# The order of ScalarE's copies where one PSUM bank is carried on into a second and a third

## The chip, the core and the metric

The kernel runs on one core of one Trainium2 chip. The metric is the device time of the whole program in microseconds (us), the median over runs. The core has five engines with queues of their own that work in program order: TensorE (PE in the profile; its weight loads are PEld), VectorE (DVE), ScalarE (ACT), GpSimd (POOL) and SyncE (SP, which here only issues DMA transfers). They wait for each other through semaphores.

## The reference

One sequence of 2048 positions and width 512 goes through a layernorm; its result feeds two branches, an attention over 8 keys at a distance of 2 with 32 heads, and a wide layer with a squared ReLU whose SiLU gates the first:

```python
xn = _layernorm(x)                               # [1, 2048, 512]
q, k, v = split(xn @ wqkv)                       # 32 heads of 16
idx = pos[:, None] - (jnp.arange(8) * 2)[None]   # keys at 0, -2, ... -14
attn = softmax(mask(q . k[idx]) * 16 ** -0.5)
s = (attn . v[idx]) @ wo
h = relu(xn @ w1 + b1) ** 2                      # width 1792
g = silu(h @ w2 + b2)
return x + s * g
```

Everything is float32.

## The kernel before

**Products.** TensorE multiplies float32 in a reduced form, so each operand is kept as a high part (ScalarE's copy into the reduced type) and a low part (VectorE's or GpSimd's subtraction of the high part from the operand), and each product is three passes: high by high, high by low, low by high. In the profile `xt`, `ss`, `w` and `h` are such pairs: a row `xt<-pxT` on ScalarE makes a high part, a row `xt<-pxT,xt` on VectorE the low one.

**Stages.** The 2048 rows are 16 tiles of 128. In the first stage each tile is normalised (`norm`, writes `xn`), spread over the partitions by four DMA transfers on SP (`shuffle`, `xb<-xn`), transposed on VectorE (`trans`, writes `pxT` for an even tile and `xs` for an odd one) and split into `xt`; then q, k and v are computed from it and stored to DRAM. The attention reads q, k and v from there and runs almost entirely on VectorE. The second stage runs the wide layer and the output product over four chunks of 512 rows. The order on all engines is written out by hand: every engine call goes through one helper on line 85, so that nearly all rows of the profile have this line and are told apart by their tiles. Attention steps are put in between by `pump`, which compares running estimates of TensorE's and VectorE's time when the program is built.

**Seven products instead of eight.** The tiles in pairs (a, a + 1) with a = 4, 6, 8, 10, 12 (`SEVEN`, line 41) compute v in the plain way (`qkv(t, 2)`, 12 matmuls, tile `pq`), but q and k together by seven products of half the depth (`seven`, line 562), 6 matmuls each. The left sides are two halves of `xt` and four sums of them, `ss`; the right sides are the weights `wq` and four sums of weights, `t`. GpSimd forms the sums of x (`sum_x`: `xs`, `xd`), after VectorE's first difference `xd<-pxT,xs`; `sum_high` (line 506) copies them to `ss` on ScalarE, and `sum_low` makes the low parts.

A first product is needed in several results. It is therefore computed once in bank X, and X is copied by ScalarE into bank Y when it holds one product and goes on by itself; Y takes another product and is copied into bank Z. These two copies are the forks of the banks. TensorE's order in a block is: X (first product, 6), v of tile a (`pq`, 12), the last product Z of the block before, X (second product, 6), v of tile a + 1 (12), Y, U, Z, Y (6 each). X's second product may not begin before the copy to Y has read the bank, and Z's product not before the copy to Z has written it.

**What stands on ScalarE beside this.** Block a also normalises tiles a + 4 and a + 5 (`first_norm`, line 738, and `second_norm`, line 742; `norm` is on line 437), as long as these exist, that is for a = 4 to 10. For tiles 6 to 15 the normalisation is one ScalarE instruction, `xn<-x,shift,rs`; its `shift` comes from GpSimd, and it writes the only buffer of `xn`, from which the four transfers of the pair before must have been read. After the second one `shuffle` issues the four transfers, and each normalisation is followed by a load of a later x on SP. `trans(t)` (line 469) ends with the copy that makes the high part of `xt`. The order around the forks is

```python
        product(X, x(a, 0), wq[0], start=True)
        first_norm(a)
        Y = psH(f"Y{a}")
        A.activation(Y, X, AF.Copy)
        second_norm(a)
```

and, further down, `trans(b + 2)` (line 605) in front of Y's next product and the copy to Z (line 609).

Of the kernel before, what the change touches and what calls it, by code (L numbers as in the profile page):

```python
# [40 lines left out]
SEVEN = range(4, 13, 2)  # L41
# [14 lines left out]
def body(ctx: ExitStack, tc: tile.TileContext, x, wqkv, wo, w1, b1, w2, b2, out):  # L56
# [48 lines left out]
    def psA(name):  # L105
        return psum.tile([P, 512], F32, name=name, tag="acc", bufs=4)

    def psH(name):
        return psum.tile([P, 512], F32, name=name, tag="h", bufs=2)

    def psT(name):
        return psum.tile([P, 512], F32, name=name, tag="tp", bufs=2)

    def piece(name):
        return keep.tile([P, 512], F32, name=name, tag="z", bufs=4)
# [248 lines left out]
    def pump(margin=-SLACK):  # L364

        limit = clock["PE"] + margin
        flush(clock["PE"])
        while True:
            if coming[0] is None:
                coming[0] = next(stream, None)  # L370
            if coming[0] is None or clock["V"] + coming[0] > limit:
                break
            coming[0] = next(stream, None)
        if coming[0] is None:
            not_before(limit)
# [61 lines left out]
    def norm(t):  # L437

        src = xins.pop(t)
        if t < TURN:  # L440
            xn[t] = dst = px.tile([P, 2, D], F32, name=f"xn{t}", tag="xb", bufs=2)[:, 0]
        else:
            if t % 2 == 0:
                xn[t] = px.tile([P, 4, 2, P], F32, name=f"xn{t}", tag="xn")
            dst = xn[t // 2 * 2][:, :, t % 2].rearrange("p a (k c) -> p k a c", k=KT)
            src = src.rearrange("p (k a c) -> p k a c", a=4, k=KT)
        if t < 6:
            halves = [slice(0, D // 2), slice(D // 2, D)] if t == 0 else [slice(None)]
            for i in halves:
                V.tensor_scalar(dst[:, i], src[:, i], mv[t][:, 0:1], rs[t], op0=OP.subtract, op1=OP.mult)  # L450
        else:
            A.activation(dst, src, AF.Identity, bias=shifts.pop(t), scale=rs[t])
        if t + 4 < NT:
            load_x(t + 4)

    def place(t):
        if t < TPC:
            xt[t] = xT[0][:, t]
        else:
            xt[t] = pxT.tile([P, 2, KT, P], FR, name=f"xt{t}", tag="xt", bufs=4)  # L460

    def shuffle(t):

        src = xn.pop(t)
        xb[t] = px.tile([P, 4, 2, P], F32, name=f"xb{t}", tag="xb", bufs=2)
        for a in range(4):
            dma(xb[t][32 * a:32 * a + 32].rearrange("p b e c -> p b (e c)"), src[:, a].rearrange("p e c -> p (e c)"))  # L467

    def trans(t):
        place(t)  # L470
        pTs[t] = piece(f"xs{t}") if t % 2 and t - 1 in SEVEN else psT(f"pxT{t}")
        if t < TURN:
            for kt in range(KT):
                PE.transpose(pTs[t][:, kt * P:(kt + 1) * P], xn[t][:, kt * P:(kt + 1) * P], ident)
            seen[t] = clock["PE"] + 800
        else:

            V.transpose(out=pTs[t].rearrange("p (k n b) -> p b k n", k=KT, b=4),
                        in_=xb[t // 2 * 2][:, :, t % 2].rearrange("p b (k c) -> p b k c", k=KT))
            seen[t] = clock["V"] + 800  # L480
        A.activation(xt[t][:, 0], pTs[t].rearrange("p (k n) -> p k n", k=KT), AF.Copy)

    def lowx(t):
        not_before(seen.pop(t))
        V.tensor_sub(xt[t][:, 1], pTs[t].rearrange("p (k n) -> p k n", k=KT), xt[t][:, 0].bitcast(F32))
        if t not in SEVEN and t - 1 not in SEVEN:
            pTs.pop(t)
# [3 lines left out]
    def sum_x(a):  # L491

        xe, t = pTs.pop(a), pTs.pop(a + 1)
        u = piece(f"xd{a}")
        V.tensor_sub(u, xe, t)
        sums[a] = t, u
        n = D // 2
        lo, hi = slice(0, n), slice(n, D)
        G.tensor_add(t[:, lo], t[:, lo], t[:, hi])
        G.tensor_sub(t[:, hi], t[:, hi], u[:, lo])  # L500
        G.tensor_add(u[:, hi], u[:, lo], u[:, hi])

    def four(ap):
        return ap.rearrange("p (s k n) -> p s k n", s=2, n=P)

    def sum_high(a):
        ss[a] = [pss.tile([P, 2, 2, 2, P], FR, name=f"ss{a}_{i}", tag="ss", bufs=2) for i in range(2)]
        for t, d in zip(sums[a], ss[a]):
            A.activation(d[:, :, 0], four(t), AF.Copy)

    def sum_low(a):
        for t, d, eng in zip(sums.pop(a), ss[a], (V, G)):
            eng.tensor_sub(d[:, :, 1], four(t), d[:, :, 0].bitcast(F32))
# [3 lines left out]
    def qkv(t, s, between=None, late=False):  # L517

        ps = (psH if t < 2 and s == 2 else psA)(f"pq{t}_{s}")
        order = [(kt, a, b) for kt in range(KT) for a, b in PASSES]  # L520
        if late:
            order.sort(key=lambda o: o[1])
        for n, (kt, a, b) in enumerate(order):
            PE.matmul(ps, xt[t][:, a, kt], wq[2 * s + kt // 2][:, b, kt % 2, :], start=n == 0, stop=n == 11)
            if between and n == 5:
                between()
        evacuate(t, s, ps)
# [9 lines left out]
    def store(t, s, stg):  # L537
        r0 = t * P + (0 if s == 0 else HALO)
        dst = (sq, sk, sv)[s][:, r0:r0 + UP, :].rearrange("g (p e) c -> p g (e c)", e=2)
        dma(dst, stg.rearrange("p g e c -> p g (e c)"))  # L540
        done = done_tiles["qkv"[s]]
        done[0] = t + 2
        done[1][t // 2] = clock["PE"]
# [18 lines left out]
    def seven(a):  # L562

        b = a + 1
        for s in (2, 0, 1):
            stgs[s] = pstg.tile([P, 4, 2, P], F32, name=f"stg{a}_{s}", tag="stg", bufs=5)
        sq_, sk_ = stgs[0], stgs[1]

        def x(t, h):
            return lambda p, k: xt[t][:, p, 2 * h + k]  # L570

        def s(i):
            return lambda p, k: ss[a][i // 2][:, i % 2, p, k]

        def product(ps, left, w, start=False, stop=False):
            n = 0
            for k in range(2):
                for p, r in PASSES:
                    PE.matmul(ps, left(p, k), w[:, r, k], start=start and n == 0, stop=stop and n == 5,
                              skip_group_check=True)  # L580
                    n += 1

        def groups(ps):
            return ps.rearrange("p (g c) -> p g c", g=4)

        X = psA(f"X{a}")
        product(X, x(a, 0), wq[0], start=True)
        first_norm(a)
        Y = psH(f"Y{a}")
        A.activation(Y, X, AF.Copy)  # L590
        second_norm(a)
        pump(LATE)
        qkv(a, 2)
        sum_high(a)
        pump(LATE)
        while tail:
            tail.pop()()
        product(X, x(a, 1), wq[1], stop=True)
        A.activation(sq_[:, :, 0], groups(X), AF.Copy, scale=0.25)
        sum_low(a)  # L600
        trans(a + 2)
        pump(LATE)
        qkv(b, 2)
        lowx(a + 2)
        trans(b + 2)
        pump(LATE)
        product(Y, s(1), tw[T2])
        Z = psH(f"Z{a}")
        A.activation(Z, Y, AF.Copy)
        U = psA(f"U{a}")  # L610
        product(U, s(0), tw[T1], start=True, stop=True)
        A.activation(sk_[:, :, 0], groups(U), AF.Copy)
        lowx(b + 2)
        if a + 2 in SEVEN:
            sum_x(a + 2)
        next_stats(a)
        pump(LATE)
        product(Z, s(2), tw[T3])
        product(Y, s(3), wq[3], stop=True)
        pump(1500)  # L620
        V.tensor_add(sk_[:, :, 1], groups(Z), sk_[:, :, 0])
        V.tensor_add(sk_[:, :, 0], groups(Y), sk_[:, :, 0])
        store(a, 1, sk_)

        def last():
            product(Z, x(b, 1), tw[T4], stop=True)
            A.activation(sq_[:, :, 1], groups(Z), AF.Copy, scale=0.25)
            store(a, 0, sq_)

        tail.append(last)  # L630
# [107 lines left out]
    def first_norm(a):  # L738
        if a + 4 < NT:
            norm(a + 4)  # L740

    def second_norm(a):
        if a + 4 < NT:
            norm(a + 5)
            shuffle(a + 4)

    def next_stats(a):
        if a + 6 < NT:
            for t in (a + 6, a + 7):
                mean(t)  # L750
                spread(t)

    for a in range(2, NT, 2):
        b, more = a + 1, a + 2 < NT
# [240 lines left out]
```

## Time and profile before

| | |
|---|---|
| median of 3 runs | 494.86 us (493.64 to 496.76) |
| the profiled execution | 495.17 us, span 493.2 us |
| first stage, by TensorE's rows | up to about 149 us of the span |
| blocks of seven, first X of each | 42.1, 60.9, 76.5, 92.1, 108.1 us |
| TensorE's granted clock, mean | 0.994 |
| waits on TensorE in the whole span | 3.3 (X for ACT's Y), 1.4 (Z for ACT's Z), 1.4, 0.4 and 0.2 us (at the start) |

A row of the timeline gives the start and the duration in us, the engine, the line, the operation, what is written and what is read (without buffer numbers), shapes and count, and, in brackets, the idle time of that engine before it with what ended it. Rows of equal neighbours are merged, so a row of six matmuls is one product. The durations of matmuls are printed with the tail of the last one. The view of the waits gives for each pair who waited and for whom, with the total, the number and the longest. The stretches by window show each engine's busy time, with the number of instructions, in a stretch of the span, and behind them the clock that TensorE was granted.

### The profile page before, as it was taken

The page shows a single profiled execution, that of the slowest core. Times are in us where ns is not written, and L with a number is a line of the kernel's source. Part 1 is how long each engine was busy: PE and PEld are TensorE (multiplying, and loading weights), DVE is VectorE, ACT ScalarE, POOL GpSimd, SP SyncE. Part 2 cuts the span into 40 slices and gives each one's busy share as a digit, 9 for nine tenths or more (in the row PEclk, how much of TensorE's full clock was granted, in tenths as well). Part 3 has the DMA queues.
Part 4 walks back from the last instruction along what each step waited for, and adds up shares of the span by engine and source line. Part 5 has one row for each costly group of instructions (what it writes and reads, how often), then busy time and mean ns, then how long its engine had stood idle before and what let it go on. Part 6 is the DMA issues. An engine that isn't in the chain of part 4 may idle for free.

```text
span 493.2 us, 5911 instructions
## 1 busy us (share of the span) xinstructions
PE 482.5 (98%) x2124; PEld 396.9 (80%) x2124; DVE 434.4 (88%) x370; ACT 227.1 (46%) x400; POOL 170.1 (34%) x149
## 2 busy tenths in 40 slices
PE   8997999999999999999999999999999999999996
PEld 5885778778888888888888888888888888888885
DVE  5996689899986999999999999899999969999543
ACT  5674555735265667229322423752233273424340
POOL 1325336422377899404140222140332213221100
PEclk9999899999999999999999999999999999999999
DMA  8799786798679964464336407471704643350222
GB/s 278 239 290 325 216 266 198 230 350 309 197 250 339 227 233 111 157 217 161 85 95 193 160 1 252 131 214 41 245 26 161 249 126 84 127 139 22 82 102 73
DMA packets 48520, 88.78 MB, mean 180 GB/s; under 512 B 5372, under 2 KB 32364, under 8 KB 45676
## 3 DMA queue, kind: packets, MB, share of 16 engines
q1 hardware_dynamic: 42444, 51.72, 33.4%
q10 hardware_dynamic: 4320, 33.56, 19.1%
q0 software_dynamic: 1728, 3.15, 4.0%
q8 instruction: 16, 0.26, 0.2%
q14 instruction: 12, 0.10, 0.1%
HBM read 57.94 MB, written 27.32 MB: 173 GB/s over the span
## 4 chain that ended last, share of the span: by engine, by line
PE 86%; DMA 4%; ACT 3%; DVE 2%; POOL 2%; issue 1%; SPq 1%; DVEq 0%; ACTq 0%; POOLq 0%
PE pb L85 31%; PE ph L85 31%; PE pq L85 10%; PE pw L85 9%; DMA xb<-xn 2%; PE Z L85 2%; DMA sk<-stg 2%; PE X L85 1%; PE Y L85 1%; POOL xs L85 1%; ACT xn L85 1%; DVE xt L85 1%; DVE xs L85 1%; SPq L467 1%; DMA x<-in_A_x 1%
## 5 line engine op out<-in xcount | busy, mean ns | idle before, releaser
L85 PE MATMUL pb<-w,h 128*128 128x512 f32 x672 | 160.6, 389 | 0.0
L85 PEld LDWEIGHTS pb<-w,h 128*128 128x128 f32 x672 | 126.1, 188 | 26.3
L85 PE MATMUL ph<-xU,w 128*128 128x512 f32 x504 | 120.6, 389 | 0.0
L85 PEld LDWEIGHTS ph<-xU,w 128*128 128x128 f32 x504 | 94.6, 188 | 19.6
L85 ACT ACTIVATE ph<-ph,b1t 128x512 f32<-128x512 f32 x56 | 37.0, 661 | 150.8 <-PE ph L85 137.3
L85 DVE TENSOR_TENSOR pv<-v,L 128x2048 f32<-128x2048 f32 x32 | 78.6, 2456 | 0.9 <-POOL L L85 0.7
L85 DVE TENSOR_TENSOR pr<-k,q 128x2048 f32<-128x2048 f32 x32 | 76.0, 2376 | 0.3
L85 DVE TENSOR_REDUCE v<-pv 128x256 f32<-128x2048 f32 x32 | 73.0, 2281 | 0.7
L85 DVE TENSOR_REDUCE L<-pr 128x128 f32<-128x2048 f32 x32 | 73.0, 2281 | 0.6
L85 POOL TENSOR_TENSOR h<-sq,h 128x512 fp32r<-128x512 f32 x15 | 25.9, 1730 | 79.6 <-ACT sq L85 76.6
L85 DVE TENSOR_TENSOR h<-ph,h 128x512 fp32r<-128x512 f32 x41 | 27.8, 679 | 22.4 <-ACT ph L85 22.3
L85 PE MATMUL pq<-wq,xt 128*128 128x512 f32 x192 | 47.2, 398 | 0.0
L85 PE MATMUL pw<-wot,oT 128*128 128x512 f32 (+1 forms) x204 | 45.9, 376 | 0.0
L85 PEld LDWEIGHTS pq<-wq,xt 128*128 128x128 f32 x192 | 37.2, 194 | 8.0
L85 PEld LDWEIGHTS pw<-wot,oT 128*128 128x128 f32 x204 | 36.8, 188 | 7.1
L85 PE MATMUL ph<-xT,w 128*128 128x512 f32 x168 | 40.4, 389 | 0.0
L85 PEld LDWEIGHTS ph<-xT,w 128*128 128x128 f32 x168 | 31.5, 188 | 6.5
L85 ACT ACTIVATE h<-ph 128x512 fp32r<-128x512 f32 x56 | 33.7, 601 | 2.5
L85 POOL TENSOR_TENSOR L<-L,mx_None 128x512 f32<-128x512 f32 x7 | 17.4, 2488 | 40.6 <-DVE mx_None L85 40.6
L85 POOL TENSOR_TENSOR w<-w1r,w 128x512 fp32r<-128x512 f32 x14 | 24.3, 1737 | 19.7 <-ACT w L85 16.9
L85 PE MATMUL pq<-wq,xT 128*128 128x512 f32 x132 | 30.8, 392 | 0.0
L85 POOL DMA_DIRECT2D z<-in_A_x x12 | 10.8, 902 | 56.3 <-DVE z L85 46.4
(103 smaller groups left out, 523.5 us busy)
## 6 DMA issues: line engine op xcount, KB each, us to landing
k<-sk ACTq DMA_DIRECT2D x8, 1408.0 KB, 6.5
v<-sv ACTq DMA_DIRECT2D x8, 1408.0 KB, 7.3
sx<-xt SPq DMA_DIRECT2D x12, 512.0 KB, 4.8
xU<-sx ACTq DMA_DIRECT2D x6, 1024.0 KB, 7.3
x<-in_A_x SPq DMA_DIRECT2D x16, 256.0 KB, 5.8
sk<-stg SPq DMA_DIRECT2D x8, 512.0 KB, 4.2
sq<-stg SPq DMA_DIRECT2D x8, 512.0 KB, 4.2
sv<-stg SPq DMA_DIRECT2D x8, 512.0 KB, 5.8
```

Of the source, the lines that this page charges most:

```text
L85: return tc.keep_in_program_order(f(*a, **k))
L467: dma(xb[t][32 * a:32 * a + 32].rearrange("p b e c -> p b (e c)"), src[:, a].rearrange("p e c -> p (e c)"))
```

## The change

It changes only the order of calls. `trans` gets an argument with which its last step, ScalarE's high part, is left to a new function `highx`; in `seven` this is used for the odd tile, whose high part is then made behind the copy to Z, in all five blocks. In the first block alone (a = 4) the copy to Y and the two copies to `ss` are put in front of both normalisations; in the others the order around Y stays.

```diff
-    def trans(t):
+    def trans(t, aside=False):
...
             seen[t] = clock["V"] + 800
+        if not aside:
+            highx(t)
+
+    def highx(t):
         A.activation(xt[t][:, 0], pTs[t].rearrange("p (k n) -> p k n", k=KT), AF.Copy)
...
         product(X, x(a, 0), wq[0], start=True)
-        first_norm(a)
+        if a > SEVEN[0]:
+            first_norm(a)
         Y = psH(f"Y{a}")
         A.activation(Y, X, AF.Copy)
+        if a == SEVEN[0]:
+            sum_high(a)
+            first_norm(a)
         second_norm(a)
         pump(LATE)
         qkv(a, 2)
-        sum_high(a)
+        if a > SEVEN[0]:
+            sum_high(a)
...
         lowx(a + 2)
-        trans(b + 2)
+        trans(b + 2, True)
         pump(LATE)
         product(Y, s(1), tw[T2])
         Z = psH(f"Z{a}")
         A.activation(Z, Y, AF.Copy)
+        highx(b + 2)
         U = psA(f"U{a}")
```

The first place is ScalarE's queue in block 4, from the first product of X on. `xn` are the normalisations of tiles 8 and 9, `ss_0` and `ss_1` the high parts of the sums, `stg_2` the evacuation of v of tile 4; the numbers at the ends of the names count buffers.

```order
-L85 ACTIVATE xn_584<-x_355,shift_544,rs_540 128x4x4x32
-L85 ACTIVATE Y_588<-X_577 128x512
-L85 ACTIVATE xn_584<-x_358,shift_551,rs_550 128x4x4x32
-L85 ACTIVATE stg_2_574<-pq_2_600 128x4x128
-L85 ACTIVATE ss_0_614<-xs_496 128x2x256
-L85 ACTIVATE ss_1_615<-xd_517 128x2x256
+L85 ACTIVATE Y_584<-X_577 128x512
+L85 ACTIVATE ss_0_586<-xs_496 128x2x256
+L85 ACTIVATE ss_1_587<-xd_517 128x2x256
+L85 ACTIVATE xn_590<-x_355,shift_544,rs_540 128x4x4x32
+L85 ACTIVATE xn_590<-x_358,shift_551,rs_550 128x4x4x32
+L85 ACTIVATE stg_2_574<-pq_2_604 128x4x128
```

The copy to Y and the two to `ss` moved in front of the two normalisations, and these stand now behind one another.

The second place is ScalarE's queue in block 6, around the copy to Z; `xt_799` is the high part of the odd tile 9, made from VectorE's transpose `xs_800`, `U_811` the bank of the next product.

```order
 L85 ACTIVATE xt_777<-pxT_778 128x512
 L85 ACTIVATE stg_2_713<-pq_2_783 128x4x128
+L85 ACTIVATE Z_808<-Y_727 128x512
 L85 ACTIVATE xt_799<-xs_800 128x512
-L85 ACTIVATE Z_809<-Y_727 128x512
 L85 ACTIVATE stg_1_715<-U_811 128x4x128
```

The copy to Z changed places with the odd high part; the same stands in blocks 4, 8, 10 and 12. On TensorE, VectorE, GpSimd and SP the order is the same before and after.

## The prediction

> **What bounds the kernel now.** I read the page first, then TensorE's waits, then the timelines around the longest of them.
>
> ```profile
> PE 482.5 (98%) x2124; PEld 396.9 (80%) x2124; DVE 434.4 (88%) x370; ACT 227.1 (46%) x400; POOL 170.1 (34%) x149
> ```
>
> TensorE is busy for 98% of the span, so only its gaps can be won, or its slow clock. The view of the waits on TensorE (us in total, times, longest) has two entries that the change touches:
>
> ```profile
> PE X L85 <- ACT Y L85: 3.3, 1, 3.3
> PE Z L85 <- ACT Z L85: 1.4, 3, 0.7
> ```
>
> Both are waits for ScalarE's copies out of a bank. The long one lies in the first block of seven products (tiles 4 and 5). TensorE's timeline there (start, us, [idle before <- releaser]):
>
> ```profile
> 42.09 1.52 PE L85 MATMUL X<-wq,xt 128*128 128x512 f32 x6
> 43.45 2.88 PE L85 MATMUL pq<-wq,xt 128*128 128x512 f32 x12
> 49.59 1.87 PE L85 MATMUL X<-wq,xt 128*128 128x512 f32 x6 [3.26 <-ACT Y L85]
> 51.26 4.32 PE L85 MATMUL pq<-wq,xt 128*128 128x512 f32 x12
> 55.42 1.55 PE L85 MATMUL Y<-t,ss 128*128 128x512 f32 x6
> 60.89 1.52 PE L85 MATMUL X<-wq,xt 128*128 128x512 f32 x6
> 62.25 2.88 PE L85 MATMUL pq<-wq,xt 128*128 128x512 f32 x12
> ```
>
> From start to start six matmuls take 1.36 (42.09 to 43.45); the printed 1.52 has a tail of 0.16, so twelve (2.88) take 2.72. Without a gap, bank X's second product would begin at 43.45 + 2.72 = 46.17 instead of 49.59. After the gap the twelve take 4.16 (51.26 to 55.42) instead of 2.72. The stretches by window (the columns after the engines' busy times are granted clock, DMA share, GB/s) say why:
>
> ```profile
> 49.50:53.00 3.50, 3.40 (x11) 2.69 (x12) 1.33 (x2) 3.04 (x7) 1.13 (x1) 0.70 1.06 382
> 53.00:56.00 3.00, 3.00 (x12) 2.40 (x11) 1.70 (x2) 0.72 (x2) 0.21 (x1) 0.79 1.05 222
> ```
>
> The clock fell after the gap: 0.30 x 3.50 + 0.21 x 3.00 = 1.7 us of work lost. From 43.45 to block 6's first X the work is 2.72 + 1.36 + 2.72 + 4 x 1.36 = 12.24, so X could start at 55.69; it starts at 60.89. The gap with its consequences costs **5.20**.
>
> **Why the copy to Y is late.** ScalarE's timeline there:
>
> ```profile
> 42.48 0.58 ACT L85 ACTIVATE stg<-pq 128x512 f32<-128x512 f32 x1
> 48.25 0.81 ACT L85 ACTIVATE xn<-x,shift,rs 128x512 f32<-128x512 f32 x1 [5.18 <-DMA sk<-stg]
> 48.97 0.57 ACT L85 ACTIVATE Y<-X 128x512 f32<-128x512 f32 x1
> 50.18 0.58 ACT L85 ACTIVATE stg<-pq 128x512 f32<-128x512 f32 x1
> 50.66 0.62 ACT L85 ACTIVATE ss<-xs 128x512 fp32r<-128x512 f32 x1
> 51.18 0.62 ACT L85 ACTIVATE ss<-xd 128x512 fp32r<-128x512 f32 x1
> 57.01 0.58 ACT L85 ACTIVATE Z<-Y 128x512 f32<-128x512 f32 x1 [0.27 <-PE Y L85]
> ```
>
> It stands idle for 5.18 in front of the normalisation xn, and Y's copy is queued behind. The page names sk<-stg as what ended it, but xn doesn't read that. It overwrites the one buffer xn, which the four transfers xb<-xn still read. The view of tile xb in the stretch 36 to 49:
>
> ```profile
> L467 SPq DMA_DIRECT2D xb<-xn x4: 552/598/622, 37.7 to 39.6; - x4
> DMA to landing us min/median/max: 4.8/8.1/8.5
> ```
>
> The last is issued at 39.6 and lands 8.5 later, at 48.1. That date the change can't move.
>
> **Part one of the change, block 4.** Y's copy needs only X's first product, whose end is 42.09 + 1.52 = 43.6; ScalarE is free from 43.1. So the copy runs 43.7 to 44.3, and TensorE goes on at 46.17. This removes the gap, and no idle stretch is left that could lower the clock: 5.20, if the rest keeps up. The two copies to ss now wait for GpSimd, and behind them the normalisations are queued, with two x loads and four xb transfers on SP that wait for these. GpSimd's rows:
>
> ```profile
> 42.37 2.84 POOL L85 TENSOR_TENSOR xs<-xs,xd 128x256 f32<-128x256 f32 x1
> 45.18 0.74 POOL L85 TENSOR_TENSOR xd<-xd 128x256 f32<-128x256 f32 x1
> 63.44 0.23 POOL L85 TENSOR_SCALAR shift<-shift 128x1 f32<-128x1 f32 x1
> ```
>
> The sums are ready at 45.2 and 45.9, so the ss copies end by 46.6. That is 1.5 ahead of 48.1: the moved copies cost nothing, hidden in ScalarE's own wait, and only a delay above 1.5 on GpSimd would reach xn. The normalisations start at 48.25 as before, the second 0.5 sooner, and so do its loads on SP; nothing waits for those. VectorE's rows:
>
> ```profile
> 44.65 2.29 DVE L85 TENSOR_REDUCE L<-pr 128x128 f32<-128x2048 f32 x1
> 53.38 0.69 DVE L85 TENSOR_TENSOR xt<-pxT,xt 128x512 fp32r<-128x512 f32 x1 [0.67 <-ACT xt L85]
> 53.98 1.09 DVE L85 STREAM_TRANSPOSE xs<-xb 128x512 f32<-128x512 f32 x1
> 57.38 0.68 DVE L85 TENSOR_TENSOR xd<-pxT,xs 128x512 f32<-128x512 f32 x1
> ```
>
> VectorE can make ss's low part from 46.9, long before Y's product at 46.17 + 1.36 + 2.72 = 50.25. What is late next is tile 6 and 7: on ScalarE two xn (0.72 each) and two stg (0.48 each) follow from 48.25, so xt's high part for tile 6 runs 50.65 to 51.25, its low part at 51.3, the odd tile's transpose 51.9 to 53.0. Bank Y's product ends at 50.25 + 1.52 = 51.8; Z's copy runs to 52.4, before TensorE asks at 52.97. Then the odd high part 53.0 to 53.6, its low part, and xd at 54.3: **3.1 sooner** than 57.38. TensorE gains 5.2 there, VectorE only 3.1.
>
> **Where the difference bites.** In blocks 6, 8 and 10 Y's copy still stands behind a normalisation, which waits for GpSimd's shift, which follows VectorE's xd. ScalarE's rows of block 6:
>
> ```profile
> 63.70 0.81 ACT L85 ACTIVATE xn<-x,shift,rs 128x512 f32<-128x512 f32 x1 [3.27 <-POOL shift L85]
> 64.42 0.58 ACT L85 ACTIVATE Y<-X 128x512 f32<-128x512 f32 x1
> 72.45 0.63 ACT L85 ACTIVATE xt<-xs 128x512 fp32r<-128x512 f32 x1 [1.24 <-DVE xs L85]
> 72.99 0.58 ACT L85 ACTIVATE Z<-Y 128x512 f32<-128x512 f32 x1
> ```
>
> Y's copy ended at 65.0 and TensorE came at 62.25 + 2.72 + 1.36 = 66.33: no wait. Moved by 3.1, the copy ends at 61.9; TensorE comes at 55.69 + 1.36 + 2.72 + 1.36 = 61.13. A **new gap of 0.8**.
>
> **Part two, the copy to Z.** It stood behind the odd tile's high part, which waits for VectorE's transpose. TensorE's rows:
>
> ```profile
> 70.41 1.52 PE L85 MATMUL Y<-t,ss 128*128 128x512 f32 x6
> 73.62 1.66 PE L85 MATMUL Z<-t,ss 128*128 128x512 f32 x6 [0.33 <-ACT Z L85]
> 76.50 1.52 PE L85 MATMUL X<-wq,xt 128*128 128x512 f32 x6
> 97.56 1.52 PE L85 MATMUL X<-wq,xt 128*128 128x512 f32 x6
> ```
>
> Y's product ends at 71.93, the transpose at 72.43, so in front the copy can start 0.5 to 1 sooner and is ready before U's end. From Y to X this block took 6.09 instead of 4 x 1.36 = 5.44: 0.65 for a wait of 0.33 (its tail 0.16 and a first product of 1.66 instead of 1.52 add to it). All three: 1.4 + 3 x 0.32, or **2.3**. The odd high part is put off at most by the copy's pitch of about 0.5, and in block 12 by the wait for Y's product; there no normalisation follows.
>
> **Block 10** has a second place for a new gap:
>
> ```profile
> 95.30 0.82 ACT L85 ACTIVATE xn<-x,shift,rs 128x512 f32<-128x512 f32 x1 [1.68 <-POOL shift L85]
> 92.32 0.69 DVE L85 TENSOR_TENSOR stg<-Y,stg 128x512 f32<-128x512 f32 x1 [0.49 <-PE Y L85]
> ```
>
> VectorE waits there for TensorE by 0.49, which falls away when TensorE leads; its lead is then 3.6, Y's copy ends at 95.30 - 3.6 + 0.72 + 0.58 = 93.0, and TensorE, 5.20 - 0.95 + 1.3 = 5.55 ahead, comes at 92.0. A new gap of 1.0.
>
> **The sum.** 5.20 + 2.3 - (0.8 + 0.15) - (1.0 + 0.15) = 5.4, with 0.15 for each first product; called 5.3, as the steps are rounded. The profiled execution lasts 495.17 (span 493.2), 0.3 above the median; I take 5.3 off the median: 494.86 - 5.3 = **489.6**. Bounds of what isn't shown: if GpSimd's sum takes 0.74, as its neighbour, not 2.84, both new gaps vanish: 7.5 in all, 487.4. If the new gaps lower the clock as the old one did, each costs 1.7 more: 493.0. I take neither: the new gaps are nearer to the old ones of Z, up to 0.7, which left the clock at 1.00 in the stretch that holds the longest of them,
>
> ```profile
> 94.00:110.00 16.00, 15.29 (x68) 12.34 (x67) 14.23 (x14) 7.64 (x14) 5.73 (x8) 1.00 1.05 340
> ```
>
> and the sum on GpSimd keeps its place behind xd and beside the same product on VectorE.
>
> **Rivals.** First, no new gaps: 487.4. For it speaks that only 0.8 and 1.0 are missing; against it that both come out of one chain of rows.
>
> Second, the slow clock isn't in every execution. X's six matmuls behind the gap take 1.67 from start to start, not far from 1.36, and only the twelve after them are slow: the stretch isn't tied to the gap's end, and the three runs before spread over 3.1 us. Where the median run lacks it, 1.7 to 1.9 of the 5.20 is no gain: 494.86 - 3.4 = 491.5. [...]
>
> Third, VectorE becomes the second bound: TensorE leads by 5.3, VectorE by 3.1 to 3.6, and in the long half TensorE would fall back to that: 491.5. Against it:
>
> ```profile
> 152.72 0.69 DVE L85 TENSOR_TENSOR h<-ph,h 128x512 fp32r<-128x512 f32 x1 [5.83 <-ACT ph L85]
> ```
>
> There VectorE waits 5.83 for work paced by TensorE, so it catches up.
>
> Fourth, the change doesn't do what it says: Y's copy still comes late, through another wait ahead of it. Only Z's 2.3 is won: 492.6. The rows show ScalarE free, so this is unlikely.
>
> Fifth, slower. Z's copy now waits for TensorE with the odd high part behind it, then VectorE's xd, GpSimd's shift, the next normalisation and the next Y. If the end of Y's product falls behind the transpose by more than the present 0.5 to 1, each block puts this loop back by a copy (0.5) and its wait, some 1 us in each of five, and all of it is lost where the first gap is not won either: about 499.9. It decides only if VectorE gains on TensorE; by the sums above it loses.
>
> **Numbers.** Forecast 0.50 (own range 488.3 to 490.9), no new gaps 0.08, clock 0.16, VectorE 0.15, no effect on Y 0.05, slower 0.06. The range 486.9 to 493.0 takes in both bounds. About 1% (4.9 us) is what a measurement of this kernel tells from no change; the forecast lies just past it, so three fifths of its chance, the first rival and a little of the others count as faster: 0.45; slower 0.06; the rest, 0.49, within 1%.
>
> **What would show it.** Right: bank X's second product near 46.2 with no idle, no low clock between 49 and 56, Y and ss ahead of xn on ScalarE with xn at 48.25; no waits of Z; a wait of X for Y near 61 and 92, around 1 us each. Wrong: xn later than 48.5 (the ss copies held it), xd not near 54.3, or waits of TensorE behind 130, which are none now.

## The result, and the profile after

The changed kernel takes 491.25 us (median of 6 runs, 490.46 to 492.60), the kernel before 495.02 beside it (6 runs, 493.64 to 496.76): a ratio of 0.9923, 95% interval 0.9898 to 0.9948. Of the 5.3 us of the forecast 3.8 came. The time lies within 1% of before, inside the wide range, but 1.65 above the predicted 489.6 and just outside the forecast's own range (488.3 to 490.9).

The profiled execution lasts 490.86, its span 489.1. TensorE's waits in it (total, times, longest):

```profile
PE X L85 <- ACT Y L85: 2.6, 2, 1.5
...
```

The waits of Z are gone, and the single wait of 3.3 of X became two that sum to 2.6. TensorE's timeline shows where they are (start, us, [idle before <- releaser]):

```profile
41.82 1.52 PE L85 MATMUL X<-wq,xt 128*128 128x512 f32 x6
...
55.43 1.52 PE L85 MATMUL X<-wq,xt 128*128 128x512 f32 x6
...
59.51 1.52 PE L85 MATMUL Z<-t,xt 128*128 128x512 f32 x6
62.20 1.65 PE L85 MATMUL X<-wq,xt 128*128 128x512 f32 x6 [1.17 <-ACT Y L85]
63.70 2.88 PE L85 MATMUL pq<-wq,xt 128*128 128x512 f32 x12
...
90.90 1.52 PE L85 MATMUL Z<-t,xt 128*128 128x512 f32 x6
93.87 1.66 PE L85 MATMUL X<-wq,xt 128*128 128x512 f32 x6 [1.46 <-ACT Y L85]
95.37 2.90 PE L85 MATMUL pq<-wq,xt 128*128 128x512 f32 x12
...
118.51 2.88 PE L85 MATMUL pq<-wq,xt 128*128 128x512 f32 x12
121.53 1.65 PE L85 MATMUL Z<-t,xt 128*128 128x512 f32 x6
123.02 5.60 PE L85 MATMUL pq<-wq,xt 128*128 128x512 f32 x24
128.46 2.88 PE L85 MATMUL ph<-xT,w 128*128 128x512 f32 x12
```

Block 4 now has no gap: from its first X to block 6's first X it takes 13.61 (41.82 to 55.43) where it took 18.80 (42.09 to 60.89). That is 5.19, against the forecast's 5.20. The losses are read from start to start. In block 6, bank X's second product begins 1.33 after the end of six matmuls from 59.51 (60.87), and its six take 1.50 instead of 1.36: 1.47 lost. In block 10 it is 1.61 + 0.14 = 1.75. In block 12, Z's tail begins 0.30 after 118.51 + 2.72 and takes 0.13 more: 0.43, which the view of the waits doesn't list. The sum is 5.20 + 2.3 - 1.47 - 1.75 - 0.43 = 3.85. From block 4's first X to the first `ph` the stretch is 86.64 now and was 90.47 (42.09 to 132.56, a row further down): 3.83. Behind the first `ph` both executions last 360.64 (489.1 - 128.46 and 493.2 - 132.56); ahead of block 4 the changed one happens to be 0.27 sooner.

The slow clock behind block 4's gap is gone as well; the two stretches that answer to those of the prediction (granted clock third from the end):

```profile
49.00:53.00 4.00, 4.00 (x20) 3.25 (x19) 1.66 (x3) 3.50 (x7) 0.00 (x0) 1.00 1.03 372
53.00:56.00 3.00, 3.00 (x15) 2.49 (x14) 2.27 (x5) 2.54 (x6) 0.62 (x1) 1.00 1.07 241
```

The mean clock of this execution is still 0.998 and not 1: it is low once more at the end of the span (0.60 from 487 to 489), behind the last matmul, where no product is left to slow down.

ScalarE's rows, block 4 first and then blocks 6 and 10:

```profile
43.38 0.58 ACT L85 ACTIVATE Y<-X 128x512 f32<-128x512 f32 x1 [0.76 <-PE X L85]
...
44.94 0.63 ACT L85 ACTIVATE ss<-xd 128x512 fp32r<-128x512 f32 x1
48.55 1.52 ACT L85 ACTIVATE xn<-x,shift,rs 128x512 f32<-128x512 f32 x2 [2.98 <-DMA sk<-stg]
...
60.86 0.81 ACT L85 ACTIVATE xn<-x,shift,rs 128x512 f32<-128x512 f32 x1 [5.00 <-POOL shift L85]
61.58 0.57 ACT L85 ACTIVATE Y<-X 128x512 f32<-128x512 f32 x1
...
92.53 0.81 ACT L85 ACTIVATE xn<-x,shift,rs 128x512 f32<-128x512 f32 x1 [2.71 <-POOL shift L85]
```

The copies to Y and to `ss` run in ScalarE's own wait and end at 45.6; the normalisations still wait for the transfers and start at 48.55 (the `sk<-stg` in the brackets was issued at 39.7 and landed 10.0 later, behind that, so it isn't what they wait for). VectorE's rows say who is late behind that:

```profile
48.49 0.73 DVE L85 STREAM_TRANSPOSE pxT<-xb 128x512 f32<-128x512 f32 x1 [1.96 <-DMA xb<-xn]
...
54.55 0.68 DVE L85 TENSOR_TENSOR xd<-pxT,xs 128x512 f32<-128x512 f32 x1
...
63.99 0.69 DVE L85 TENSOR_TENSOR ss<-xs,ss 128x512 fp32r<-128x512 f32 x1 [0.58 <-ACT ss L85]
...
86.08 0.69 DVE L85 TENSOR_TENSOR xd<-pxT,xs 128x512 f32<-128x512 f32 x1
...
88.64 0.69 DVE L85 TENSOR_TENSOR stg<-Y,stg 128x512 f32<-128x512 f32 x1
89.25 2.28 DVE L85 TENSOR_TENSOR pv<-v,L 128x2048 f32<-128x2048 f32 x1
...
95.66 0.69 DVE L85 TENSOR_TENSOR ss<-xs,ss 128x512 fp32r<-128x512 f32 x1 [1.80 <-ACT ss L85]
...
120.81 0.67 DVE L85 TENSOR_TENSOR stg<-Z,stg 128x512 f32<-128x512 f32 x1
```

And of before, the rows of VectorE, and behind them the row of TensorE, that these are measured against:

```profile
89.37 0.68 DVE L85 TENSOR_TENSOR xd<-pxT,xs 128x512 f32<-128x512 f32 x1
...
123.11 0.67 DVE L85 TENSOR_TENSOR stg<-Z,stg 128x512 f32<-128x512 f32 x1
```

```profile
132.56 0.62 PE L85 MATMUL ph<-xT,w 128*128 128x512 f32 x2
```

VectorE leads its old times by 2.83 at block 4's `xd` (57.38 to 54.55), by 3.29 at block 8's (89.37 to 86.08), and by 2.30 at block 12's evacuation of Z (123.11 to 120.81). TensorE leads by 5.46 at block 6's first X (60.89 to 55.43) and by 4.10 at the first `ph`. What TensorE has above VectorE it gives back, at Y's copies and then at Z's tail.

### The profile page after: what moved, and what is told of

The parts are those of the page before. It is cut to its first block, busy times and chain, and to the rows that moved or that the text cites. A ratio compares the mean times of both kernels' runs of the same rounds, so it can differ in the third digit from the quotient of the medians.

```text
span 489.1 us, 5913 instructions
## 1 busy us (share of the span) xinstructions
PE 480.4 (98%) x2124; PEld 395.7 (81%) x2124; DVE 432.1 (88%) x370; ACT 227.0 (46%) x400; POOL 166.4 (34%) x149
## 4 chain that ended last, share of the span: by engine, by line
PE 78%; DVE 7%; DMA 6%; issue 2%; POOL 2%; ACT 2%; SPq 1%; DVEq 0%; POOLq 0%; ACTq 0%
PE pb L85 31%; PE ph L85 31%; PE pw L85 9%; PE pq L85 6%; DMA xb<-xn 3%; DMA sk<-stg 2%; DVE L L85 1%; DMA x<-in_A_x 1%; DVE pr L85 1%; POOL xs L85 1%; DVE xt L85 1%; ACT xn L85 1%; POOL rs L85 1%; SPq L467 1%; DVE stg L85 1%
## 5 line engine op out<-in xcount | busy, mean ns | idle before, releaser
L85 DVE TENSOR_TENSOR pv<-v,L 128x2048 f32<-128x2048 f32 x32 | 76.5, 2391 | 0.9 <-POOL L L85 0.7
L85 POOL TENSOR_TENSOR h<-sq,h 128x512 fp32r<-128x512 f32 x15 | 24.3, 1621 | 89.2 <-ACT sq L85 83.9
L85 PE MATMUL pq<-wq,xt 128*128 128x512 f32 x192 | 45.8, 389 | 0.0
L85 PEld LDWEIGHTS pq<-wq,xt 128*128 128x128 f32 x192 | 36.0, 188 | 7.5
L85 POOL TENSOR_TENSOR L<-L,mx_None 128x512 f32<-128x512 f32 x7 | 19.6, 2793 | 40.1 <-DVE mx_None L85 40.1
L85 POOL TENSOR_TENSOR w<-w1r,w 128x512 fp32r<-128x512 f32 x14 | 25.8, 1842 | 20.6 <-ACT w L85 19.6
L85 PEld LDWEIGHTS pq<-wq,xT 128*128 128x128 f32 x132 | 24.5, 188 | 5.8 <-ACT xT L85 0.7
```

The lines of the kernel that those rows point to most:

```text
L85: return tc.keep_in_program_order(f(*a, **k))
```

## The experiments

Two theories were set against each other. A: the order of ScalarE's copies alone makes TensorE's gaps, and each gap that is removed is a gain. B: from block 6 on VectorE's chain (transposes, differences, and through GpSimd the shift) sets the pace, TensorE's gaps only show where it meets this chain, and a gap that goes at one place comes back at another.

One measure serves for all of them: the time from block 4's first X to the first `ph`. It leaves out what executions differ by ahead of block 4 (its first X starts at 41.6 to 43.8 from one execution to the next).

**Before once more**, with no edit.

> The kernel before, unchanged, to see whether the slow stretch of TensorE's clock behind the first gap is there in every execution. Theory (it belongs to the gap): every run shows a mean clock near 0.994, as the profiled one did, and the stretch of about 3.4 us at half speed stands between 49 and 55 us. Rival (it is there in some executions only): some runs show 0.997 or more and are about 1.7 us shorter than the others. Time 494 to 496 in both.

Measured: 494.67 (10 runs), ratio 1.0006, 0.9988 to 1.0024. In its profile:

```profile
49.22 2.92 PE L85 MATMUL X<-wq,xt 128*128 128x512 f32 x6 [3.20 <-ACT Y L85]
```

```profile
49.00:53.00 4.00, 3.78 (x10) 3.02 (x11) 1.33 (x2) 3.24 (x7) 1.34 (x1) 0.57 1.00 360
...
```

The gap of 3.20 is there again, and the low clock too, but it lies in another place: here over bank X's second product, in the first profile over the twelve matmuls behind it. Of the 33 runs of the kernel before that were taken together with it, 7 had a mean clock of 0.999 or 1.0 and took 493.2 to 494.6; the other 26 had 0.991 to 0.997 and took 494.1 to 497.1. In the 64 runs of the change and of the versions below that keep the copy to Y in front in block 4, one has 0.997 and the others 0.998 to 1.0, so a mean of 0.997 or less stands for the slow stretch with few exceptions. It is in most executions, not in all: the rival holds.

**Part one alone** (block 4).

```diff
-        trans(b + 2, True)
+        trans(b + 2)
...
-        highx(b + 2)
```

> Only the first part: in block 4 the copies to Y and ss stand ahead of both normalisations, while all odd high parts stay ahead of the copy to Z. Theory (the chain VectorE, GpSimd's shift, normalisation leads by about 3 us and TensorE falls back to it wherever it is tied to it): Z's copy in block 4 now waits for VectorE's transpose, a gap of about 1.7 there; the Z gaps of blocks 6 to 10 stay; the time ends at about 492.2, so that the second part of the change is worth about 1. Rival (the parts add up): 5.2 less with both new gaps, that is about 493.5, since the second part would have been worth its own 2.3.

Measured: 491.87 (6 runs, 491.23 to 492.25), ratio 0.9933, 0.9916 to 0.9949. TensorE's waits and rows:

```profile
PE Z L85 <- ACT Z L85: 3.7, 4, 1.5
```

```profile
54.20 1.66 PE L85 MATMUL Z<-t,ss 128*128 128x512 f32 x6 [1.48 <-ACT Z L85]
...
```

The forecast of 492.2, with a gap of 1.7 in block 4, held (1.48 came). Nearly the whole gain stands with part one. The waits of Z grew from 1.4 to 3.7, since TensorE now reaches them sooner; with part two these 3.7 become 2.6 for Y. No wait for Y is left here: the delay sits at Z instead.

**Part two alone** (the copy to Z).

```diff
-        if a > SEVEN[0]:
-            first_norm(a)
+        first_norm(a)
...
-        if a == SEVEN[0]:
-            sum_high(a)
-            first_norm(a)
...
-        if a > SEVEN[0]:
-            sum_high(a)
+        sum_high(a)
```

> Only the second part: the copy to Z stands ahead of the odd high part in all blocks, while the order around Y in block 4 is as before. Theory: the first gap and the slow clock stay, the three waits for Z vanish, about 2.0 is won of 2.3 (a short new wait for Y in block 10): 493.0. Rival (VectorE is the second bound all along): the waits return elsewhere, 494.5 to 495.

Measured: 496.83 (12 runs, 493.92 to 498.15), ratio 1.0025, 1.0006 to 1.0044. The 2.3 of this part did not come; it is slightly slower, and neither the 493.0 nor the 494.5 to 495 of the rival came. The profile is of its shortest run, in which the clock stayed at full speed behind a gap of 3.43:

```profile
49.64 1.65 PE L85 MATMUL X<-wq,xt 128*128 128x512 f32 x6 [3.43 <-ACT Y L85]
...
59.29 1.52 PE L85 MATMUL X<-wq,xt 128*128 128x512 f32 x6
...
96.95 1.66 PE L85 MATMUL X<-wq,xt 128*128 128x512 f32 x6 [1.88 <-ACT Y L85]
...
131.53 0.84 PE L85 MATMUL ph<-xT,w 128*128 128x512 f32 x3
```

```profile
49.00:53.00 4.00, 3.36 (x15) 2.79 (x16) 1.33 (x2) 3.54 (x8) 1.08 (x1) 1.00 1.00 359
```

The waits of Z are gone, and from block 6's first X to the first `ph` it still takes 72.24 (59.29 to 131.53) where before took 71.67 (60.89 to 132.56): from start to start 2.18 are given back in block 10 (1.88 of idle, which before had none), 0.44 at Z's tail and 0.24 in block 6. This is theory B. One cause is in block 4: the copy to Z waits 0.76 there for Y's product, the odd high part stands behind it (from 55.91, though VectorE's transpose ended at 55.11), and VectorE waits 1.45 for that, up to 56.56, where it waits 0.70 in the other blocks. What makes the median 2.9 longer than this run is open: the other runs have mean clocks of 0.990 to 0.997, which points to slow stretches, but they have no profile.

**The copy to Y ahead of the first normalisation in all blocks.**

```diff
-        if a > SEVEN[0]:
-            first_norm(a)
...
-            first_norm(a)
+        first_norm(a)
```

> The changed kernel, and the copy to Y ahead of the first normalisation in all blocks, not in block 4 alone. Theory A (the two new gaps of 1.5 and 1.75 in blocks 6 and 10 are lost time of TensorE alone): they vanish and the time is 491.25 - 3.2 = 488.0. Theory B (VectorE's chain sets the pace from block 6 on, the gap is only the place where TensorE meets it): both gaps vanish, but TensorE waits as long in block 12, where the last product of Z needs VectorE's sum out of Z, and the time stays at 490.8 to 491.3.

Measured: 491.22 (6 runs, 490.73 to 491.80), ratio 0.9921, 0.9905 to 0.9937: the same as the change. TensorE's waits:

```profile
PE Z L85 <- DVE stg L85: 2.5, 3, 1.4
```

Not one wait for Y is left, and the 2.6 came back as 2.5 of waits at Z's tail, for VectorE's evacuation. By theory A 3.2 would have been won. A falls.

**GpSimd's shift ahead of the sums of x.** The statistics of the next pair stand ahead of the sums.

```diff
+        next_stats(a)
         if a + 2 in SEVEN:
             sum_x(a + 2)
-        next_stats(a)
```

> The changed kernel with the statistics of the next pair (VectorE's row sums, GpSimd's shift) ahead of the sums of x of block a + 2. Theory B (VectorE's chain sets the pace of the blocks from 6 on, and its own waits and long rows decide the end): GpSimd's shift of 128 x 1 no longer falls beside VectorE's product pv and takes about 0.2 instead of 2.27, the normalisation and with it the copy to Y in block 10 come about 1.8 sooner, in block 6 about 0.6 sooner (no wait for the sum xs), so TensorE's waits for the copy to Y shrink from 2.6 to under 1 in all: 488.9. Theory A (TensorE's order of copies alone decides, the place of the gap is free to move): the waits only move to another copy, 491.2, as they did with the copy to Y in front in all blocks.

Measured: 490.68 (7 runs, 489.81 to 492.89), ratio 0.9922, 0.9890 to 0.9954. The waits for Y are gone, but the time is 0.6 below the change, not 2.4, and the intervals overlap: nearer to theory A's number, though the wait went to VectorE and not to another copy:

```profile
122.28 1.65 PE L85 MATMUL Z<-t,xt 128*128 128x512 f32 x6 [1.17 <-DVE stg L85]
```

A shift that comes sooner doesn't shorten VectorE's chain, and in this order the statistics even stand ahead of VectorE's `xd` (block 4's comes 13.25 behind the first X, with the change 12.73 and 12.19 in its two profiles). GpSimd's long row didn't vanish either, it moved to the second normalisation's `rs` (2.60 at 91.14, beside VectorE's `pv` from 91.05). My 488.9 took the shift for the chain.

**Copies to Y and to `ss` ahead of both normalisations in all blocks.**

```diff
-        if a > SEVEN[0]:
-            first_norm(a)
...
-        if a == SEVEN[0]:
-            sum_high(a)
-            first_norm(a)
+        sum_high(a)
+        first_norm(a)
...
-        if a > SEVEN[0]:
-            sum_high(a)
```

> The changed kernel with the copy to Y and the two copies to ss ahead of both normalisations in all blocks, not in block 4 alone. Theory B: VectorE's own waits for ss (0.58 in block 6, 1.80 in block 10) vanish, its chain is up to 2.4 sooner, no wait for Y stays; the normalisations come later, and the shuffles behind them, but the buffers have slack there: 489.3. Rival: the later normalisation puts back the next pair's transposes by the two copies (1.2 in a block), VectorE waits for the transfers instead, and the time stays at 491.2 or rises to 492.

Measured: 489.14 (6 runs, 488.25 to 490.77), ratio 0.9896, 0.9867 to 0.9926. The theory's 489.3 holds. VectorE's waits for `ss` are gone:

```profile
63.66 0.68 DVE L85 TENSOR_TENSOR ss<-xs,ss 128x512 fp32r<-128x512 f32 x1
...
69.43 0.69 DVE L85 TENSOR_TENSOR xt<-xs,xt 128x512 fp32r<-128x512 f32 x1 [0.70 <-ACT xt L85]
```

VectorE no longer waits 0.58 and 1.80, 2.4 in all, and the time is 2.1 below the change. It is as much below the version with only the copy to Y in front in all blocks (491.22), from which this one differs by the copies to `ss` alone. VectorE's one wait left in a block is the 0.70 for the odd tile's high part.

**The copies to `ss` of block 4 where they stood before**, only the copy to Y in front.

```diff
-            sum_high(a)
...
-        if a > SEVEN[0]:
-            sum_high(a)
+        sum_high(a)
```

> The changed kernel, but in block 4 only the copy to Y goes ahead of the normalisations; the two copies to ss stand where they stood before. By the steps of the prediction, the ss copies would then run behind both normalisations and the evacuation of v, at about 50.6, their low parts at 51.5, and TensorE would wait for them about 1.2 at Y's second product (50.0): a gap moves to there. If that wait counts in full, 491.25 + 1.2 = 492.4. Theory B: VectorE sets the pace behind, the wait only takes away lead which TensorE would lose in blocks 6 to 12 anyway: 491.3, with TensorE's waits for Y in block 6 and 10 smaller by about as much.

Measured: 492.40 (12 runs, 490.96 to 494.92), ratio 0.9956, 0.9938 to 0.9973. The first of the two numbers expected came, 492.4, and not 491.3:

```profile
52.84 1.99 PE L85 MATMUL Y<-t,ss 128*128 128x512 f32 x6 [0.74 <-ACT ss L85]
...
65.56 1.65 PE L85 MATMUL X<-wq,xt 128*128 128x512 f32 x6 [1.18 <-ACT Y L85]
...
```

A new gap at `ss`, and the two for Y as long as with the change (1.18 here, 1.45 in block 10). For theory B as I had worked it out this is a miss: I forgot that the two copies then stand ahead of the high part of tile 6, which VectorE waits for,

```profile
52.17 0.62 ACT L85 ACTIVATE ss<-xs 128x512 fp32r<-128x512 f32 x1
...
54.26 0.60 ACT L85 ACTIVATE xt<-pxT 128x512 fp32r<-128x512 f32 x1 [0.46 <-DVE pxT L85]
```

so that VectorE's chain is put back by about as much as TensorE (block 4's `xd` comes 14.12 behind the first X instead of 12.73, and block 6's first X 15.00 instead of 13.61: 1.39 for both), and none of it is hidden. The moved copies to `ss` are a needed part of the change.

**The normalisations of block 4 behind the evacuation of v**, so that tile 6's high part stands right behind the first of them.

```diff
         if a == SEVEN[0]:
             sum_high(a)
-            first_norm(a)
-        second_norm(a)
+        else:
+            second_norm(a)
...
+        if a == SEVEN[0]:
+            first_norm(a)
         trans(a + 2)
+        if a == SEVEN[0]:
+            second_norm(a)
```

> The changed kernel, but in block 4 the two normalisations, which can't start before 48.5, stand behind the evacuation of v, just ahead of the transpose of tile 6 and the second one behind that tile's high part, so that the high part no longer waits for both of them and for stg. Theory B: the high part of tile 6 is made at about 49.6 instead of 50.9, VectorE's xd about 1.2 sooner, so the waits for Y in block 6 and 10 shrink from 1.17 and 1.46 to about 0.3 each and Z's tail in block 12 isn't late: 488.7. Rival: another chain (the shuffles behind the second normalisation, or VectorE's own work) is as late, and the time stays at 491.2.

Measured: 490.22 (6 runs, 489.57 to 491.58), ratio 0.9914, 0.9889 to 0.9939: 1.0 below the change where 2.5 were expected, with overlapping intervals. The wait in block 6 is gone (0.23 are lost there from start to start), that of block 10 is not:

```profile
94.62 1.67 PE L85 MATMUL X<-wq,xt 128*128 128x512 f32 x6 [1.42 <-ACT Y L85]
```

Block 10's gap has a cause of its own, on GpSimd (below).

**The change once more**, with no edit.

> The changed kernel once more, unaltered, beside the two versions of this call: 491.25 as before, within 0.5. Its runs show how much of the spread comes from ahead of the blocks: between executions the first block of seven products began at 41.8 or at 43.8, with the weights' first transfers.

Measured: 491.85 (6 runs, 490.26 to 493.32), ratio 0.9927, 0.9902 to 0.9952: 0.6 above the first 491.25, where within 0.5 was expected, and no other than part one alone (491.87). In the profiled execution the last transfer of tiles 6 and 7 landed 0.74 sooner than in the first (VectorE's transpose started at 47.75 instead of 48.49), while block 4 began 0.20 sooner, so the chain behind it gained 0.54, and the gap of block 6 is smaller by about that:

```profile
59.30 1.52 PE L85 MATMUL Z<-t,xt 128*128 128x512 f32 x6
61.47 1.66 PE L85 MATMUL X<-wq,xt 128*128 128x512 f32 x6 [0.64 <-ACT Y L85]
```

0.81 from start to start (61.47 - 60.66), where it was 1.33 and the prediction had 0.8.

**VectorE's wait filled.** The version with Y and `ss` ahead, and VectorE's row statistics of tiles 10 and 12 put into the 0.70 of blocks 4 and 6.

```diff
         highx(b + 2)
+        for t in (a + 6, a + 7):
+            if t < NT and t in STATS:
+                row_stats(t)
         U = psA(f"U{a}")
```

> The version with the copies to Y and to ss ahead of both normalisations in all blocks, and VectorE's row statistics of tiles 10 and 12 (0.68 each) moved into the 0.70 in which VectorE waits for the odd tile's high part, in blocks 4 and 6. Theory B (VectorE's chain sets the pace behind block 4): VectorE is 0.6 sooner behind block 4 and 1.2 behind block 6, the late tail of Z in block 12 (0.74 idle, 0.9 in all) and the 0.35 lost in block 8 vanish: 489.14 - 1.25 = 487.9. Theory A (only the order of ScalarE's copies counts): nothing changes on ScalarE, 489.1.

Measured: 488.62 (4 runs, 487.30 to 489.86), ratio 0.9862, 0.9836 to 0.9887. It lies between the two numbers, and the interval doesn't tell it from the version without the fill. Z's tail is on time; one wait of 0.55 for the copy to Z came up in block 10, behind a normalisation that was late there, since GpSimd's `rs` took 2.66 (at 91.58) beside VectorE's `pv`.

**Both together**: the fill, and block 4's normalisations behind the evacuation of v.

```diff
         sum_high(a)
-        first_norm(a)
-        second_norm(a)
+        if a > SEVEN[0]:
+            first_norm(a)
+            second_norm(a)
...
+        if a == SEVEN[0]:
+            first_norm(a)
         trans(a + 2)
+        if a == SEVEN[0]:
+            second_norm(a)
```

> The same with the two normalisations of block 4 behind the evacuation of v, so that the high part of tile 6 comes about 0.4 sooner. If TensorE has no gap left in the version without this, nothing is to be had: 487.9, the same within 0.4. If VectorE's chain still leaves a gap there, up to 0.4 less: 487.5; at 488.5 or more the later second normalisation and the shuffles behind it hold the next pair.

Measured: 487.87 (5 runs, 487.11 to 490.51), ratio 0.9855, 0.9825 to 0.9885: the 487.9 that was expected, and the fastest of all. Its interval lies below that of the change, but overlaps that of the version without the later normalisations. TensorE's waits in the whole span are two, both at the start:

```profile
PE warm L85 <- POOL ident masks.py:199: 1.3, 1, 1.3
PE pxT L85 <- DVE xn L85: 0.7, 1, 0.7
```

Here is the stretch with hardly a gap: 41.69 to 124.73, 83.04. In order of the median:

| kernel | first X of block 4 to first ph | median |
|---|---|---|
| part two alone | 89.56 | 496.83 |
| before | 90.47 | 495.02 |
| before once more | 90.35 | 494.67 |
| copies to ss behind | 88.05 | 492.40 |
| part one alone | 87.83 | 491.87 |
| the change (two profiles) | 86.64, 86.08 | 491.25, 491.85 |
| Y first in all blocks | 87.37 | 491.22 |
| statistics first | 85.37 | 490.68 |
| normalisations of block 4 late | 85.35 | 490.22 |
| Y and ss first in all blocks | 84.26 | 489.14 |
| the same, wait filled | 83.80 | 488.62 |
| both together | 83.04 | 487.87 |

But for part two alone, whose profile is of its shortest run, for Y first in all blocks and for the second profile of the change, the medians fall with the stretch, by 7.15 against 7.43 from before to the last: the rest of the program takes little of the gains back. In three profiles it takes some: TensorE waits 0.40 (copies to `ss` behind), 0.95 (statistics first) and 0.98 (wait filled) for GpSimd's `h`, at 225.6 to 230.8. Neighbours in this table mostly have overlapping intervals; the last and the change have not.

## Why the prediction was right, and where its size was off

**Block 4** went as written: the gap and the slow clock are gone, 5.19 of 5.20, the copies to `ss` end 3.0 ahead of the normalisations, these start at 48.55 (48.25 was said, and later than 48.5 was named as a sign of being wrong; but it was the transfers that held them, VectorE's transpose of the same transfers starts at 48.49), and `xd` comes 2.83 sooner (3.1 was said). "TensorE gains 5.2 there, VectorE only 3.1" was the right reading. That the two copies to `ss` must move, and cost nothing there, is shown by the version that leaves them behind: its stretch is 1.41 longer than the change's (88.05 against 86.64), its median 1.15.

**Part two** removes the waits of Z, as said: from Y to block 8's first X block 6 takes 5.44, as without a gap. But "2.3" as a term of its own is right only while TensorE is ahead of nobody. Alone it brought nothing, on top of part one 0.6 by one measurement of the change and nothing by the other (491.87 to 491.25 and 491.85, intervals overlapping), though the stretch is 1.19 and 1.75 shorter. The sum came out near because the losses were counted apart.

**The new gaps** are where the prediction put them and for the reason it gave, but they were mis-sized: 1.47 and 1.75 for 0.95 and 1.15. The 0.52 of block 6 are 0.25 by which the copy to Y ended later (62.15 for 61.9, as the normalisations of block 4 started 0.30 later and `xd` came at 54.55 for 54.3), and 0.26 by which TensorE came sooner (60.87 for 61.13, the 0.27 from ahead of block 4). In the second profile of the change, with an earlier landing, this gap has the predicted size, while the wait in block 10 stays at 1.42: what was off in block 6 is how executions differ, what was off in block 10 is not.

In block 10 the step that failed is "its lead is then 3.6". VectorE's evacuation does lead by 3.68 (92.32 to 88.64), but the shift doesn't follow from the evacuation: it follows from `xd`, whose lead is 3.29. Then GpSimd lost another 0.52. Its rows of the change:

```profile
89.32 2.27 POOL L85 TENSOR_SCALAR rs<-rs 128x1 f32<-128x1 f32 x1
...
92.58 0.19 POOL L85 TENSOR_SCALAR rs<-rs 128x1 f32<-128x1 f32 x1
```

And of before:

```profile
92.61 0.19 POOL L85 TENSOR_SCALAR rs<-rs 128x1 f32<-128x1 f32 x1
...
93.52 1.75 POOL L85 TENSOR_TENSOR shift<-mean,rs 128x1 f32<-128x1 f32 x1
```

In the change the first `rs`, one number per partition, takes 2.27; its twin at 92.58 takes 0.19. It starts 0.07 behind VectorE's product `pv` (89.25 to 91.53) and ends 0.06 behind it. Before, VectorE's wait of 0.49 for TensorE let `rs` and the next operation start ahead of the product, and the third, the shift, took 1.75; from `rs` to the normalisation it was 2.69 (92.61 to 95.30), now it is 3.21 (89.32 to 92.53). The lead of 3.29 for 3.6 and these 0.52 make 0.83; TensorE, held longer in block 6, came at 92.26 for 92.0, which takes back 0.25, and 0.6 are left, as measured (1.75 for 1.15). The long `rs` is no accident of one execution: it took 2.26 with the normalisations late and with Y and `ss` first in all blocks, 2.25 in part two alone, each time begun 0.07 or 0.08 behind the start of the same product and ended 0.05 behind its end. The wait that the prediction was glad to see fall away had let `rs` run ahead of the product. That the row takes 2.25 to 2.27 beside the product and 0.19 without it is measured; what links the two engines there isn't shown.

**Z's tail in block 12**, 0.43, was in no term: "The odd high part is put off at most by the copy's pitch" looked at ScalarE's queue, while what came late was VectorE's evacuation of Z (it ended at 121.48, TensorE was there at 121.23). It is the third rival in small.

**The rivals.** By the number alone the second and the third rival, both 491.5, were nearer to 491.25 than the forecast; the profile tells them apart. The third, VectorE as the second bound, holds, but not as priced. I looked for it in the long half; there VectorE still has slack (no wait of TensorE behind 130, as said, and both executions take 360.64 there). It decides inside the blocks, from 6 to 12, and takes 3.65 of the 7.5 that both parts are worth. That the gaps are VectorE's and not the copies' is shown by two versions: Y in front everywhere leaves the time at 491.22 with the gap at Z's tail, and taking away VectorE's own waits wins 2.1. The second rival is true in part: the slow stretch is not in every execution of before, but in 26 of 33, so the median has it, and its 1.7 counted. The first, no new gaps, is what the last version is: 83.04 against 90.47, a gain of 7.43, where the prediction's two terms made 7.5. The change doesn't reach it. The fourth fell with the profile. Of the fifth, part two alone shows a trace: the loop that was priced at 1 us in each of five blocks is there in block 4, where VectorE waits 0.75 longer. In the change it isn't: from block 4 to 10 ScalarE's odd high part waits 0.78 to 1.23 for VectorE's transpose, and so doesn't stand late behind the copy to Z. Why the median of part two alone is 0.25% above before stays open.

## What to carry to other kernels

When a gap on the busiest engine goes, write down the lead that each other engine gets at each later meeting point, from which row it starts, and the slack that it had there; the smallest sum of the two, not the gap, bounds the gain up to there. In block 6 the copy to Y leads by 2.85 (65.0 to 62.15) and had 1.33 of slack (65.0 to 66.33): 4.18, and TensorE's second X leads by 4.13 (66.33 to 62.20). Moving a copy only moves the gap if another engine's chain is the late one: look for that engine's own short waits (0.58, 0.70 and 1.80 here) and fill or remove these; here removing 0.58 and 1.80 won 2.1, and what filling the 0.70 won can't be told from none. And read the times of a gap from start to start, with the first instruction behind it: the view of the waits showed 2.6 of the 3.65 lost here.

## What the runs showed of the hardware

The clock doesn't follow from the length of a gap alone. With a gap of 3.20 and one of 3.26 it fell (0.43 x 4.00 = 1.7 us lost in the one, 1.7 in the other as the prediction worked it out); with one of 3.43, in the profile of part two alone, it stayed at 1.00. In two profiles of one kernel the slow stretch lies differently against the gap's end: in the first of before it begins 1.28 behind it (49.59 to 50.87), X's six matmuls take 1.67 from start to start and the twelve behind them 4.16; in the second the six take 2.73 (49.22 to 51.95) and the twelve 3.00.

In length the two agree. In stretches of 0.1 us the clock is 0.50 from 50.87 to 54.28 in the first profile of before, 3.41 in all. For the second, an estimate: 0.57 from 49 to 53 makes 0.43 x 4.00 / 0.50 = 3.4, if the clock was 0.50 there too (from 45 to 49 and from 53 to 56 it was 1.00). Behind the last matmul it is 0.50 once more, from 491.19 to the end of the span at 493.2 in the first profile of before, and from 487.4 to 489.1 with the change. What decides whether a gap of this length lowers the clock, and when, isn't shown: the three gaps show only that a like one costs 1.7 by the clock in one execution and nothing in another.

An execution's start moves by 2 us: block 4 began at 41.6 to 42.1 in ten profiles, and at 43.8 in three. That is half of what the change wins, so a single run of each kernel wouldn't have told them apart.
